# The first MLP product of a spectral MLP kernel, computed as seven block products of 256 tokens

## The chip, the cores and the metric

The kernel runs on one core of one Trainium2 chip. The metric is device time in microseconds; several executions of the same program are timed, and the median is given. One further execution is recorded by the hardware profiler. Its engines are PE (TensorE, the matrix multiplier; its weight loads are listed apart as PEld), DVE (VectorE), ACT (ScalarE), POOL (GpSimd) and SP (SyncE, which issues transfers). Each engine runs its own queue of instructions in order and waits on the others by semaphores. All matmul results land in PSUM, which has eight banks of 512 float32 columns on 128 partitions; ACT and DVE read them from there.

## The reference

The reference takes eight sequences of 3008 tokens with 256 features through a spectral filter, and then every token through an MLP of two layers (hidden width 2048, leaky ReLU):

```python
X = np.fft.rfft(x, axis=1)
Yr = Xr @ w_r - Xi @ w_i + b_r
Yi = Xr @ w_i + Xi @ w_r + b_i
# soft threshold 0.01 on both, then
y = np.fft.irfft(Y, n=x.shape[1], axis=1)
...
h = x @ w_in                    # x: 24064 x 256, w_in: 256 x 2048
g = np.maximum(0.01 * h, h)
return (g @ w_out)              # w_out: 2048 x 256
```

## The kernel before

The Fourier transform of length 3008 = 47 x 64 is done by matmuls. For each of the eight sequences (`b`) there are three stages, which hand on through DRAM: `fwd(b)` (transform of length 47: load `xin`, fold, multiply by `fa`, store to `u_dram`), `mid(b)` (transform of length 64 by `fb` in `stage_b`, the two complex products with the filter in `proj`, soft threshold, back by `gb` in `stage_g`, store to `v_dram`) and, inside the MLP, `inverse` (back transform of length 47 by `ga`). For accuracy every float32 operand is split into a high and a low part (`_hi`, `_lo`, `gh`, `gl`, `yh`, `yl`: the high part is a cast to float32r, the low part the rest), and every product is done by three matmuls: high by high, high by low, low by high (`products`). The weights `w_in` and `w_out` come as float64 bits and are converted on chip (`convert_win`, `load_wout`).

The MLP works on chunks of two column sets: 52 chunks, 44 of them of 470 tokens and 8 of 423 (padded to 424). For each chunk and each of 16 blocks of 128 hidden features (`f`) the function `moe_h` does the first product (six matmuls into one PSUM bank named `psh`), ACT applies the leaky ReLU from PSUM into `gf` (L437) and casts it to `gh` (L438), and DVE forms `gl` (L439). `moe_o` does the second product (six matmuls, L455) three blocks later (`LAG = 3`), accumulating over all 16 blocks into two banks named `pso`. During a chunk, `v_load` and `inverse` make the next chunk's tokens.

The PSUM banks are given out in rotation by name: `psh` has two, `pso` three, `psf` (all other stages) three. The code interleaves the other stages with the MLP by generators: a `Stream` of `fwd(b + 2)` and one of `mid(b + 1)` are advanced a little after each step of the MLP. The code's order is not the final one: a scheduler of the language puts the instructions of each engine in an order of its own, from its own estimates of times, when the program is built. The order then is fixed, and each engine follows it. Ahead of the MLP lie `fwd(0)`, `mid(0)` and `fwd(1)`, and the conversion of the weights; I call this the start.

## Time and profile before

| | |
|---|---|
| Time, median of 3 runs (lowest to highest) | 2699.18 us (2699.11 to 2699.51) |
| Profiled execution: time, span of its instructions | 2699.9 us, 2698.1 us |
| Mean granted TensorE clock | 0.995 |
| PE busy, matmuls recorded | 2651.5 us (98%), 13848 |
| DVE busy, instructions | 1329.4 us (49%), 2447 |
| ACT busy, instructions | 1421.9 us (53%), 2781 |
| POOL busy, instructions | 225.7 us (8%), 180 |
| Mean transfer rate | 61 GB/s |

A matmul's record lasts from its start to its last result, and the next one starts well before that; what a matmul costs in a dense row is therefore the distance from its start to the next start, not its duration. A line of the profile that names a helper (L76, `products`) stands for all its callers, which the tile names tell apart: `psh<-yh,win_hi` is the first MLP product, `pso<-gh,wout_hi` the second. The profiled execution lies 1.8 us above its span and 0.7 us above the median of the timed runs.

### The profile page before, as it was taken

The numbers are of one execution on the slowest core, as the hardware profiler recorded it, in microseconds if no ns is written. First come the engines' busy times: TensorE is split into PE (matmuls) and PEld (weight loads), VectorE is DVE, ScalarE is ACT, GpSimd is POOL, SyncE is SP. The second block draws the span as 40 slices with busy tenths as digits, with TensorE's granted clock in tenths as the row PEclk, the third lists the DMA queues.
The fourth block names the chain that finished last, engine by engine and source line by source line (L and its number), as shares of the span: only waits on it lengthen the run. The fifth ranks groups of instructions, "written<-read, shape, count | busy, mean of one in ns | idle before, by whom it ended". The sixth has DMA issues, their size and how long they took to land.

```text
span 2698.1 us, 36477 instructions
## 1 busy us (share of the span) xinstructions
PE 2651.5 (98%) x13848; PEld 2379.0 (88%) x13848; DVE 1329.4 (49%) x2447; ACT 1421.9 (53%) x2781; POOL 225.7 (8%) x180
## 2 busy tenths in 40 slices
PE   5899999999999999999999999999999999999999
PEld 3688989988898988998889888898889989899888
DVE  6685653555445554455544555445543454433232
ACT  4465555555555555555554555555555555545454
POOL 0011110111101111011100011001000000000000
PEclk8999999999999999999999999999999999999999
DMA  7732222122211212122121221212212011110000
GB/s 221 207 108 64 68 60 69 56 65 59 61 52 56 66 51 71 43 70 61 52 64 42 68 71 48 70 45 67 57 39 60 26 46 39 38 39 27 8 15 14
DMA packets 121260, 164.74 MB, mean 61 GB/s; under 512 B 13697, under 2 KB 83325, under 8 KB 121085
## 3 DMA queue, kind: packets, MB, share of 16 engines
q1 hardware_dynamic: 80640, 116.07, 13.9%
q10 hardware_dynamic: 40445, 46.34, 6.9%
q8 instruction: 109, 1.79, 0.3%
q14 instruction: 66, 0.54, 0.1%
HBM read 86.60 MB, written 75.76 MB: 60 GB/s over the span
## 4 chain that ended last, share of the span: by engine, by line
PE 96%; DMA 1%; DVE 1%; ACT 1%; issue 0%; SPq 0%; ACTq 0%; DVEq 0%
PE psh L76 39%; PE pso L455 39%; PE psf L76 12%; PE psf L407 3%; PE psf L285 3%; PE pso L285 0%; DMA xin<-x_dram 0%; DMA u<-u_dram 0%; PE pso L76 0%; DMA raw<-w_out_dram 0%; ACT xin L233 0%; DMA w_r<-w_r_dram 0%; DMA u_dram<-xin 0%; DVE zf L337 0%; DMA fa<-fa_dram 0%
## 5 line engine op out<-in xcount | busy, mean ns | idle before, releaser
L439 DVE TENSOR_TENSOR gl<-gf,gh 128x470 fp32r<-128x470 f32 (+1 forms) x832 | 557.6, 671 | 1055.0 <-ACT gh L438 978.5
L437 ACT ACTIVATE gf<-psh 128x470 f32<-128x470 f32 (+1 forms) x832 | 464.1, 558 | 847.7 <-PE psh L76 787.1
L76 PE MATMUL psh<-yh,win_hi 128*128 128x470 f32 (+1 forms) x1664 | 636.0, 382 | 0.0
L455 PE MATMUL pso<-gh,wout_lo 128*128 128x470 f32 (+1 forms) x1664 | 621.6, 374 | 0.0
L76 PE MATMUL psh<-yl,win_hi 128*128 128x470 f32 (+1 forms) x1664 | 618.7, 372 | 0.0
L76 PE MATMUL psh<-yh,win_lo 128*128 128x470 f32 (+1 forms) x1664 | 618.2, 371 | 0.0
L455 PE MATMUL pso<-gh,wout_hi 128*128 128x470 f32 (+1 forms) x1664 | 617.3, 372 | 0.0
L455 PE MATMUL pso<-gl,wout_hi 128*128 128x470 f32 (+1 forms) x1664 | 604.2, 372 | 4.5 <-DVE gl L439 4.5
L438 ACT CAST gh<-gf 128x470 fp32r<-128x470 f32 (+1 forms) x832 | 483.3, 581 | 25.3 <-ACT gf L437 3.9
L455 PEld LDWEIGHTS pso<-gl,wout_hi 128*128 128x128 f32 x1664 | 312.4, 188 | 41.4 <-DVE gl L439 4.9
L455 PEld LDWEIGHTS pso<-gh,wout_hi 128*128 128x128 f32 x1664 | 312.9, 188 | 37.3
L76 PEld LDWEIGHTS psh<-yh,win_lo 128*128 128x128 f32 x1664 | 313.3, 188 | 35.9
L455 PEld LDWEIGHTS pso<-gh,wout_lo 128*128 128x128 f32 x1664 | 313.1, 188 | 36.0
L76 PEld LDWEIGHTS psh<-yh,win_hi 128*128 128x128 f32 x1664 | 314.0, 189 | 31.2
L76 PEld LDWEIGHTS psh<-yl,win_hi 128*128 128x128 f32 x1664 | 315.7, 190 | 28.9
L319 POOL TENSOR_TENSOR kb<-bias,kc 128x512 f32<-128x512 f32 x84 | 110.8, 1319 | 1437.3 <-ACT kc L316 1350.4
L329 DVE TENSOR_TENSOR t<-psf,kb 64x256 f32<-64x256 f32 x336 | 141.5, 421 | 28.1 <-PE psf L76 24.4
L407 PEld LDWEIGHTS psf<-ga,vin 120*128 120x128 f32 x832 | 116.5, 191 | 12.1 <-issue 4.4
L407 PE MATMUL psf<-ga,vin 120*128 120x128 f32 x832 | 118.0, 275 | 2.5 <-DMA vin<-v_dram 2.4
L212 POOL TENSOR_TENSOR xs<-xin,xin 120x512 f32<-120x512 f32 (+1 forms) x42 | 55.7, 1327 | 564.3 <-DMA xin<-x_dram 327.6
L421 DVE TENSOR_TENSOR yl<-y,yh 128x470 fp32r<-128x470 f32 (+1 forms) x104 | 72.3, 696 | 61.3 <-ACT yh L420 61.0
L345 ACT ACTIVATE zh<-t,sign 128x256 fp32r<-128x256 f32 x168 | 76.7, 503 | 47.8 <-DVE t L331 46.5
(121 smaller groups left out, 2500.5 us busy)
## 6 DMA issues: line engine op xcount, KB each, us to landing
u<-u_dram SPq DMA_DIRECT2D x192, 128.0 KB, 2.7
v_dram<-v ACTq DMA_DIRECT2D x192, 128.0 KB, 2.4
vin<-v_dram SPq DMA_DIRECT2D x96, 240.0 KB, 3.3
xin<-x_dram SPq DMA_DIRECT2D x90, 240.0 KB, 3.0
out_dram<-ob SPq DMA_DIRECT2D x88, 235.0 KB, 2.3
u_dram<-xin ACTq DMA_DIRECT2D x72, 240.0 KB, 2.4
u_dram<-xin SPq DMA_DIRECT2D x24, 240.0 KB, 6.4
win_raw<-w_in_dram SPq DMA_DIRECT2D x4, 1024.0 KB, 7.7
```

The lines of the kernel that those rows point to most:

```text
L76: last = nc.tensor.matmul(dst, a, b, start=(i == 0), stop=(i == len(terms) - 1))
L212: eng.tensor_add(xs, xa, xb)
L285: nc.tensor.matmul(pv[:, dh, :, i, :], u[:, i, s], fbt[:, 0:k + 2:k + 1, :], start=True, stop=True)
L319: pool.tensor_add(kb, bias, kc.unsqueeze(1).broadcast_to([P, 2, D]))
L329: dve.tensor_add(t[64 * r:64 * (r + 1), i, :], ps_y[s, r * D:(r + 1) * D], kb[s, r, :])
L345: act.mul(zh[:, i, :], t[:, i, :], s)
L407: nc.tensor.matmul(py[:, o:o + P], vin[:, c, i, s], consts["ga"][:, c, :], start=True, stop=True)
L421: last = dve.tensor_sub(yl[:, eh, :n], y[:, :n], yh[:, eh, :n].bitcast(F32))
L437: act.activation(gf[:, :n], ph[:, :n], AF.Prelu, alpha=SLOPE)
L438: act.copy(gh[:, :n], gf[:, :n])
L439: dve.tensor_sub(gl[:, :n], gf[:, :n], gh[:, :n].bitcast(F32))
L455: nc.tensor.matmul(po[:, :n], a[:, f, s], r[:, :n], start=(f == 0 and j == 0), stop=(f == NF - 1 and j == 2),)
```

## The change

The first MLP product is regrouped. Chunks now have 512 tokens (47 chunks, which no longer fall together with the column sets, now called pairs). Hidden features are taken two blocks at a time (`q`, 8 steps a chunk). For one step the product of a 2 x 2 block matrix of weights (two blocks of hidden features by two halves of the 256 input features) and a 2 x 2 block matrix of tokens (two halves of the features by two halves of 256 tokens) is computed by seven block products instead of eight. The sums of weight blocks are formed once in `convert_win` (seven forms, `[P, 7, NQ, P]`), the sums of token blocks once per chunk in `forms`. Each block product is three matmuls with 256 columns. With the products called P1 to P7, `moe_a` puts P1 and P6 into the two halves of one bank and P5 and P7 into those of another; ACT copies P1 out (`p1`), DVE adds `u2` = P1 + P6 and `c22` = P7 + `u2` + P5. Then `moe_b` lets TensorE add P2 onto P1, P3 onto P5 and P4 onto P7, and DVE adds `u2` to the latter two. ACT applies the leaky ReLU in three pieces, casts all 1024 columns to `gh`, and DVE forms `gl`. `moe_o` is the second product as before, with 512 columns, and two steps of lag.

PSUM now has three `psh` banks and two `pso` banks; each step takes two `psh` banks, so the first bank of a step is the second bank of the step two before. Many SBUF tiles of different stages now share buffers (one name per group: `e`, `z`, `u`, `v`, `y`, `yc`, `yl`, `gf`, ...). Two of these matter below: the first two input tiles of `fwd(1)` lie in the buffers of `yc`, which `inverse` and `forms` fill and read for the first two chunks; and the output tile `ob`, the tile `y` of `inverse` and the tile `v` of `stage_g` share two buffers. The streams of `fwd` and `mid` are now advanced one after the other, at a rate that spreads them over 95% of a sequence's share of the chunks instead of 75%.

The core of the diff:

```diff
     NPAIR = NK1 // 2
-    NT = 2 * NG * N1
+    NQ = NF // 2
+    NT, HT = 512, 256
+    NV = 2 * NG * N1
...
+    def block(dst, l, r, start=False):
+        for i, (a, b) in enumerate(((l[0], r[0]), (l[0], r[1]), (l[1], r[0]))):
+            nc.tensor.matmul(dst, a, b, start=start and i == 0, stop=i == 2, skip_group_check=True)
...
     def convert_win(c):
         if c == 0:
-            pair("win", [P, NH, DF])
-        s = slice(c * NIN, (c + 1) * NIN)
-        float64_parts(win_raw[c], *(w[:, :, s] for w in consts["win"]), (("vin", 2), ("raw", 3)))
+            pair("win", [P, 7, NQ, P])
+        a, q = float64_parts(win_raw[c], (("vin", 2), ("yh", 2)))
+        dve.tensor_add(a, a, q)
+        a = a.rearrange("p (j q i m) -> p j q i m", j=NH, q=2, i=2)
+        a11, a12, a21, a22 = (a[:, j, :, i] for i in range(2) for j in range(2))
+        s = sb.tile([P, 4, 2, P], F32, name="ws", tag="yh", bufs=2)
+        dve.tensor_add(s[:, 0], a21, a22)
+        dve.tensor_sub(s[:, 2], a11, a21)
+        dve.tensor_sub(s[:, 1], s[:, 0], a11)
+        dve.tensor_sub(s[:, 3], a12, s[:, 1])
+        hi, lo = (w[:, :, 2 * c:2 * c + 2] for w in consts["win"])
+        for k, w in ((slice(0, 2), a[:, :, :, 0]), (2, a22), (slice(3, 7), s)):
+            act.copy(hi[:, k], w)
+            last = dve.tensor_sub(lo[:, k], w, hi[:, k].bitcast(F32))
+        return last
...
-            while len(raws) < min(c + 2 if c < 2 else c + 3, NF // n):
-                raw = sb.tile([P, CS, 2], U32, name="raw", tag="raw", bufs=3)
+            while len(raws) < min(c + 2 if c < 2 else c + 4, NF // n):
                 k = len(raws)
+                raw = sb.tile([P, CS, 2], U32, name="raw", tag="ez"[k % 2])
                 with tc.issue_after(reads[-1].ins):
                     sync.dma_start(raw.rearrange("p (a f) w -> p a (f w)", a=n), ov[:, k * n:(k + 1) * n, :])
...
-            s = slice(c * n, (c + 1) * n)
-            made.append(float64_parts(raws[c], *(w[:, s, :] for w in consts["wout"]), (("cva", 2), ("cvq", 1))))
+            a, q = float64_parts(raws[c], (("u", 3), ("v", 2)))
+            dh, dl = (w[:, c * n:(c + 1) * n, :] for w in consts["wout"])
+            a, q = (t.rearrange("p (a f) -> p a f", a=n) for t in (a, q))
+            act.copy(dh, a)
+            dve.tensor_sub(a, a, dh.bitcast(F32))
+            made.append(dve.tensor_add(dl, a, q))
...
-    XT = [(("xa", 3), ("xb", 3))] * 3 + [(("yh", 2), ("gh", LAG + 1)), (("yl", 2), ("gh", LAG + 1))] * 2
-    XT1 = XT[:3] + [(("gh", LAG + 1),) * 2] * 2 + [(("gl", LAG + 1),) * 2] * 2
+    XT = [("gf", 1)] + [("gl", 2)] * 2 + [("gh", 2)] * 2 + [("yc", 2)] * 2
+    XT1 = [("yc", 2)] * 2 + [("gf", 1)] + [("gh", 2)] * 2 + [("gl", 2)] * 2
...
+        lo = p0[pi]
+        while lo < p0[pi + 1]:
+            ci = lo // NT
+            hi = min((ci + 1) * NT, p0[pi + 1])
+            if ci not in f_t:
+                f_t[ci] = sb.tile([P, NH, NT], F32, name="yc", tag="yc")
+            act.copy(f_t[ci][:, eh, lo - ci * NT:hi - ci * NT], y[:, lo - p0[pi]:hi - p0[pi]])
+            lo = hi
...
+    def forms(ci):
+        y = f_t.pop(ci)
+        b11, b12, b21, b22 = (y[:, j, k * HT:(k + 1) * HT] for j in range(2) for k in range(2))
+        t = sb.tile([P, 2, HT], F32, name="yt", tag="yt", bufs=1)
+        yh, yl = y_t[ci] = tuple(sb.tile([P, 7, HT], F32R, name=n_, tag=n_) for n_ in ("yh", "yl"))
+        def split(k, w):
+            act.copy(yh[:, k], w)
+            return dve.tensor_sub(yl[:, k], w, yh[:, k].bitcast(F32))
+        split(0, b11)
+        split(slice(1, 3), y[:, 1].rearrange("p (k n) -> p k n", k=2))
+        dve.tensor_sub(t[:, 0], b12, b11)
+        dve.tensor_sub(t[:, 1], b22, t[:, 0])
+        dve.tensor_sub(b12, b22, b12)
+        dve.tensor_sub(b11, b21, t[:, 1])
+        split(slice(3, 5), t)
+        last = split(slice(5, 7), y[:, 0].rearrange("p (k n) -> p k n", k=2))
+        if ci == 0:
             made[:] = [last]
-    def moe_h(ci, f):
-        n = t0[ci + 1] - t0[ci]
-        n += n % 2
-        s = slice(f * P, (f + 1) * P)
-        ph = bank("psh", 2)
-        products(ph[:, :n], [
-            (tuple(w[:, kt, s] for w in consts["win"]), tuple(y[:, kt, :n] for y in y_t[ci]))
-            for kt in range(NH)
-        ])
-        gf = sb.tile([P, NT], F32, name="gf", tag="gf")
-        gh = sb.tile([P, NT], F32R, name="gh", tag="gh", bufs=LAG + 1)
-        gl = sb.tile([P, NT], F32R, name="gl", tag="gl", bufs=LAG + 1)
-        act.activation(gf[:, :n], ph[:, :n], AF.Prelu, alpha=SLOPE)
-        act.copy(gh[:, :n], gf[:, :n])
-        dve.tensor_sub(gl[:, :n], gf[:, :n], gh[:, :n].bitcast(F32))
-        g_t[ci, f] = (gh, gl)
...
+    AK = (0, 1, 6, 2, 3, 4, 5)
+    BK = (0, 1, 2, 5, 3, 4, 6)
+    def product(dst, ci, q, k, start=False):
+        block(
+            dst, tuple(w[:, AK[k - 1], q] for w in consts["win"]), tuple(y[:, BK[k - 1]] for y in y_t[ci]), start)
+    def moe_a(ci, q):
+        b1, b2 = bank("psh", 3), bank("psh", 3)
+        lo, hi = slice(0, HT), slice(HT, NT)
+        product(b1[:, lo], ci, q, 1, True)
+        product(b1[:, hi], ci, q, 6)
+        product(b2[:, hi], ci, q, 7, True)
+        product(b2[:, lo], ci, q, 5)
+        p1 = sb.tile([P, HT], F32, name="p1", tag="p1", bufs=1)
+        u2 = sb.tile([P, HT], F32, name="u2", tag="u2", bufs=1)
+        act.copy(p1, b1[:, lo])
+        dve.tensor_add(u2, b1[:, hi], p1)
+        c22 = sb.tile([P, HT], F32, name="c22", tag="p1", bufs=1)
+        dve.tensor_add(c22, b2[:, hi], u2)
+        dve.tensor_add(c22, b2[:, lo], c22)
+        h_t[ci, q] = (b1, b2, u2, c22)
+    def moe_b(ci, q):
+        b1, b2, u2, c22 = h_t.pop((ci, q))
+        lo, hi = slice(0, HT), slice(HT, NT)
+        product(b1[:, lo], ci, q, 2)
+        product(b2[:, lo], ci, q, 3)
+        product(b2[:, hi], ci, q, 4)
+        g = sb.tile([P, 4, HT], F32, name="gf", tag="gf", bufs=1)
+        act.activation(g[:, 3], c22, AF.Prelu, alpha=SLOPE)
+        act.activation(g[:, 0], b1[:, lo], AF.Prelu, alpha=SLOPE)
+        dve.tensor_add(
+            g[:, 1:3], b2.rearrange("p (k n) -> p k n", k=2), u2.unsqueeze(1).broadcast_to([P, 2, HT]))
+        act.activation(g[:, 1:3], g[:, 1:3], AF.Prelu, alpha=SLOPE)
+        gh = sb.tile([P, 4, HT], F32R, name="gh", tag="gh")
+        act.copy(gh, g)
+        gl = sb.tile([P, 4, HT], F32R, name="gl", tag="gl")
+        dve.tensor_sub(gl, g, gh.bitcast(F32))
+        g_t[ci, q] = (gh, gl)
...
+        if q == 0:
+            o_t[ci, eh] = bank("pso", 2)
+        po = o_t[ci, eh]
+        s = slice(eh * P, (eh + 1) * P)
+        for i in range(2):
+            f = 2 * q + i
             for j, (a, r) in enumerate(((wh, gh), (wl, gh), (wh, gl))):
...
+        if q == NQ - 1:
+            ob = sb.tile([P, NT], F32, name="ob", tag="y")
+            act.copy(ob, po)
+            sync.dma_start(out[s, ci * NT:(ci + 1) * NT], ob)
...
-        for i, (ci, f) in enumerate(steps):
-            moe_h(ci, f)
+        for i, (ci, q) in enumerate(steps):
+            moe_a(ci, q)
             if i >= LAG:
-                moe_o(*steps[i - LAG])
+                moe_o(*steps[i - LAG], 0)
+            yield ci + (q + 0.5) / NQ
+            if i >= LAG:
+                moe_o(*steps[i - LAG], 1)
+            moe_b(ci, q)
...
```

Three places show how the change moves instructions. The first is PE in the last chunk, where only the MLP is left. Before, the six matmuls of one first product (the last three are shown) are followed by a second product (numbers tell tiles of one name apart):

```order
L76 MATMUL psh_25152<-yh_24741,win_hi_234 128x424
L76 MATMUL psh_25152<-yl_24742,win_hi_234 128x424
L76 MATMUL psh_25152<-yh_24741,win_lo_235 128x424
L455 MATMUL pso_24935<-gh_25122,wout_hi_739 128x424
L455 MATMUL pso_24935<-gh_25122,wout_lo_740 128x424
L455 MATMUL pso_24939<-gh_25122,wout_hi_739 128x424
L455 MATMUL pso_24939<-gh_25122,wout_lo_740 128x424
L455 MATMUL pso_24935<-gl_25123,wout_hi_739 128x424
```

Now, at the same place, the last product of a step (P4, into `psh_28720`) is followed at once by the first product (P1) of the step two later, into `psh_28821`, which lies in the same bank; P2 of the step between comes behind it:

```order
L84 MATMUL psh_28720<-yh_28391,win_hi_216 128x256
L84 MATMUL psh_28720<-yl_28392,win_hi_216 128x256
L84 MATMUL psh_28720<-yh_28391,win_lo_217 128x256
L84 MATMUL psh_28821<-yh_28391,win_hi_216 128x256
L84 MATMUL psh_28821<-yl_28392,win_hi_216 128x256
L84 MATMUL psh_28821<-yh_28391,win_lo_217 128x256
...
L84 MATMUL psh_28770<-yh_28391,win_hi_216 128x256
L84 MATMUL psh_28770<-yl_28392,win_hi_216 128x256
L84 MATMUL psh_28770<-yh_28391,win_lo_217 128x256
```

What moved: between the last write of a `psh` bank and its first write two steps later PE has nothing else in its queue here; before, a whole second product lay between.

The second place is DVE in the same chunk. Before, DVE has only one instruction for each block of 128 hidden features:

```order
L439 TENSOR_TENSOR gl_25085<-gf_25083,gh_25084 128x424
L439 TENSOR_TENSOR gl_25104<-gf_25102,gh_25103 128x424
L439 TENSOR_TENSOR gl_25123<-gf_25121,gh_25122 128x424
L439 TENSOR_TENSOR gl_25142<-gf_25140,gh_25141 128x424
L439 TENSOR_TENSOR gl_25161<-gf_25159,gh_25160 128x424
```

Now it has five instructions for each step (two blocks):

```order
L503 TENSOR_TENSOR gf_28710<-psh_28669,u2_28683 128x512
L487 TENSOR_TENSOR u2_28734<-psh_28719,p1_28733 128x256
L509 TENSOR_TENSOR gl_28717<-gf_28710,gh_28715 128x1024
L489 TENSOR_TENSOR c22_28737<-psh_28720,u2_28734 128x256
L490 TENSOR_TENSOR c22_28737<-psh_28720,c22_28737 128x256
L503 TENSOR_TENSOR gf_28761<-psh_28720,u2_28734 128x512
L487 TENSOR_TENSOR u2_28785<-psh_28770,p1_28784 128x256
```

What moved: the `gl` of one step (`gl_28717`) stands in the queue between `u2` and `c22` of the next one, so that `c22` waits for it, and with `c22` the products P3 and P4.

The third place is DVE at the end of the start. Before, the additions of `fwd(1)` on the input tiles stand ahead of the additions of `inverse` (`y`) for the first chunks:

```order
L212 TENSOR_TENSOR xs_847<-xin0_799,xin1_801 120x512
L213 TENSOR_TENSOR xin0_799<-xin0_799,xin1_801 120x512
L212 TENSOR_TENSOR xs_858<-xin0_803,xin1_805 120x512
L213 TENSOR_TENSOR xin0_803<-xin0_803,xin1_805 120x512
L212 TENSOR_TENSOR xs_869<-xin0_807,xin1_809 120x256
L213 TENSOR_TENSOR xin0_807<-xin0_807,xin1_809 120x256
L414 TENSOR_TENSOR y_764<-psf_756,odd_763 128x240
L416 TENSOR_TENSOR y_764<-psf_756,odd_763 128x230
```

Now they stand behind `inverse` and `forms` (`yl`) of the first two chunks and the first two conversions of `w_out` (`wout_lo`), directly ahead of the first MLP step's `u2`:

```order
L233 TENSOR_TENSOR xs_876<-xin_847 120x512
L234 TENSOR_TENSOR xin_844<-xin_844 120x512
L234 TENSOR_TENSOR xin_847<-xin_847 120x512
L233 TENSOR_TENSOR xs_887<-xin_850 120x512
L234 TENSOR_TENSOR xin_850<-xin_850 120x512
L233 TENSOR_TENSOR xs_898<-xin_853 120x512
L234 TENSOR_TENSOR xin_853<-xin_853 120x512
L233 TENSOR_TENSOR xs_909<-xin_856 120x512
L234 TENSOR_TENSOR xin_856<-xin_856 120x512
L233 TENSOR_TENSOR xs_920<-xin_859 120x256
L234 TENSOR_TENSOR xin_859<-xin_859 120x256
L487 TENSOR_TENSOR u2_992<-psh_977,p1_991 128x256
```

What moved: from the first conversion of `w_out` to the first `u2` DVE now has 62 instructions in a row, the 14 of `fwd(1)` last.

More of the change, by code (lines that the diff above doesn't have):

```diff
@@ L240, in fwd @@
             load(c)
-        yield 0
+        yield 4 * CS if b >= NPRE else 0
         fold(0)
@@ L278, in stage_b @@
             u = u_t.pop(j)
-            pb = bank("pso", 3) if b < 1 else bank("psf", 3)
+            pb = bank("psh", 3) if b < 1 else bank("psf", 3)
             pv = pb.rearrange("p (a c i k) -> p a c i k", a=NH, c=2, i=2)
@@ L350, in stage_g @@
         def stage_g(j):
-            pg = bank("pso", 3) if b < 1 else bank("psf", 3)
+            pg = bank("psh", 3) if b < 1 else bank("psf", 3)
             last = products(pg, [(consts["gb" if b else "gb32"], tuple(flat(z) for z in z_t.pop(j)))])
@@ L478, in moe @@
         for s in steps[-LAG:]:
-            moe_o(*s)
+            for eh in range(NH):
+                moe_o(*s, eh)
     class Stream:
@@ L641, in _tokens @@
     cols = []
[L642 removed]
+    for c in _pairs(nb):
         n2 = [(b, NS * g + s) for b, s, n in c for g in range(n)]
```

227 lines of the change are left out of this document (106 added, 121 removed).

## The prediction

> **What bounds the kernel now.** I read the page first: shares of the span, slices, the chain that ended last.
>
> ```profile
> span 2698.1 us, 36477 instructions
> PE 2651.5 (98%) x13848; PEld 2379.0 (88%) x13848; DVE 1329.4 (49%) x2447; ACT 1421.9 (53%) x2781; POOL 225.7 (8%) x180
> ...
> PEclk8999999999999999999999999999999999999999
> ...
> PE 96%; DMA 1%; DVE 1%; ACT 1%; issue 0%; SPq 0%; ACTq 0%; DVEq 0%
> ```
>
> PE carries the time: 98% busy, 96% of the chain, at full clock after the first slice. Whether it is dense shows in the windows (length; busy time of PE, PEld, DVE, ACT, POOL; clock; share and rate of transfers):
>
> ```profile
> 0.00:50.00 50.00, 26.61 (x79) 14.97 (x80) 28.21 (x39) 23.86 (x36) 0.52 (x5) 0.83 0.87 274
> 50.00:100.00 50.00, 41.92 (x198) 33.26 (x197) 39.73 (x74) 23.62 (x51) 0.00 (x0) 0.93 0.60 167
> 100.00:150.00 50.00, 38.69 (x154) 26.12 (x153) 37.16 (x68) 25.82 (x53) 5.86 (x5) 0.97 0.66 205
> ...
> 1000.00:1500.00 500.00, 500.00 (x2652) 454.25 (x2650) 241.51 (x453) 265.11 (x524) 48.98 (x39) 1.00 0.20 58
> ```
>
> In the middle PE never idles, and DVE is half busy (241.51 of 500). Only the start has holes. So the time is the MLP's matmuls, and less work on PE is worth its full length as long as nothing else makes PE wait.
>
> **PE work.** Distances between starts in the timeline (start, duration):
>
> ```profile
> 1501.06 0.28 PE L76 MATMUL psf<-wn_hi,eh 128*128 128x256 f32 x1
> ...
> 1501.78 0.37 PE L76 MATMUL psh<-yh,win_hi 128*128 128x470 f32 x1
> ...
> 1503.05 0.38 PE L455 MATMUL pso<-gh,wout_hi 128*128 128x470 f32 x1
> ...
> 1508.30 0.39 PE L76 MATMUL psf<-zh,gb_hi 128*128 128x512 f32 x1
> ...
> 1508.98 0.38 PE L76 MATMUL psh<-yh,win_hi 128*128 128x470 f32 x1
> ```
>
> Six matmuls lie between the first rows: 0.72/6 = 0.120 us with 256 columns; 1.27/6 = 0.212 with 470; three with 512 take 0.68/3 = 0.227. The line through 256 and 470 gives 0.230 at 512 and 0.192 at 424; I take 0.230. Before, the MLP has 44 chunks x 16 x 12 = 8448 matmuls of 470 columns and 1536 of 424: 1791 + 295 = 2086 us. After, 47 chunks x 8 steps x 21 = 7896 of 256 and 4512 of 512: 948 + 1038 = 1986. The change takes off 100 us. Bounds: 0.227 for 512 columns makes it 114, 0.233 makes it 87. All lies on the path. The seven products save an eighth of half the MLP, some 130 us; about 30 go back to the fixed part of twice as many short matmuls.
>
> A short product needs as many weight loads as a long one:
>
> ```profile
> L76 PEld LDWEIGHTS psf<-wn_hi,eh 128*128 128x128 f32 x168 | 31.6, 188 | 2.0
> ```
>
> The load lasts 188 ns, longer than 120, yet the rows above run at 0.120: loads overlap. The Trainium skill ("TensorE: Matmul & The Clock Gate", LDWEIGHTS) gives a load of 128 columns 107 ns. By it a 256-column product is not held up, but any shorter one would be; the 0.120 agrees with that.
>
> **Vector work.** Rows of the nearest forms (busy, mean ns | idle before):
>
> ```profile
> L439 DVE TENSOR_TENSOR gl<-gf,gh 128x470 fp32r<-128x470 f32 x704 | 479.7, 682 | 894.7 <-ACT gh L438 883.0 <-PE psh L76 3.8 <-PE pso L455 3.4
> L298 DVE TENSOR_TENSOR xi<-psf,xi 128x256 f32<-128x256 f32 x84 | 35.7, 425 | 49.2 <-ACT eh L297 46.7
> L299 DVE TENSOR_TENSOR el<-psf,eh 128x512 fp32r<-128x512 f32 x84 | 57.2, 681 | 0.0
> L134 DVE TENSOR_TENSOR win_lo<-cva,cvq 128x1024 fp32r<-128x1024 f32 x4 | 4.9, 1219 | 0.0
> L221 DVE CAST xh<-xin 120x512 fp32r<-120x512 f32 x36 | 22.8, 634 | 11.5 <-PE psf L76 11.1
> L316 ACT COPY kc<-psf 128x256 f32<-128x256 f32 x96 | 35.8, 373 | 38.8 <-PE psf L76 38.0
> L95 ACT CAST wd_hi<-w_d 128x512 fp32r<-128x512 f32 x1 | 0.6, 621 | 0.0
> L132 ACT CAST win_hi<-cva 128x1024 fp32r<-128x1024 f32 x4 | 4.2, 1056 | 4.9 <-DVE cva L128 4.8
> L455 PE MATMUL pso<-gl,wout_hi 128*128 128x470 f32 x1408 | 517.0, 375 | 4.5 <-DVE gl L439 4.5
> ```
>
> DVE per step: `u2` and two `c22` 3 x 0.425, the addition into `gf` 0.681, `gl` 1.219: 3.18 us against 5.28 of PE (21 x 0.120 + 12 x 0.230). That is 376 x 3.18 = 1194 us instead of 558. `forms` adds four subtractions (0.425) and 0.425 + 3 x 0.681 of splits, 4.2 us a chunk or 196; the splits of `inverse` (72 us) go. DVE comes to some 2100 us, 80%. ACT: 0.373 (`p1`), 0.4 and 0.373 and 0.621 (ReLU), 1.056 (cast) are 2.8 a step, 1060 us for 948; with the copies to `yc` and `forms` some 1650, 63%. Neither engine is full over any chunk (some 42 of DVE against 54 of PE), so I cost this throughput at nothing, with PE as its cover. `forms` stands in the queue almost a chunk ahead of its use. What does cost is latency.
>
> **New waits in the steady part.** The handovers, at one block of the MLP:
>
> ```profile
> 2502.42 0.37 PE L76 MATMUL psh<-yh,win_lo 128*128 128x470 f32 x1
> ...
> 2502.83 0.56 ACT L437 ACTIVATE gf<-psh 128x470 f32<-128x470 f32 x1 [1.60 <-PE psh L76]
> ...
> 2503.42 0.59 ACT L438 CAST gh<-gf 128x470 fp32r<-128x470 f32 x1
> ...
> 2504.04 0.65 DVE L439 TENSOR_TENSOR gl<-gf,gh 128x470 fp32r<-128x470 f32 x1 [2.13 <-ACT gh L438]
> ```
>
> An engine starts 0.03 to 0.04 us after the one that it waits for; a 256-column result is there 0.28 - 0.12 = 0.16 after PE went on. Two chains start at P4, the last product of a step:
> - To the bank: 0.16 + 0.04 + 0.68 (addition into `gf`, which empties the bank) + 0.06 back to PE = 0.94 us until P1 of the step two later may write there.
> - To the second product: 0.16 + 0.04 + 0.68 + 0.04 + 0.62 (ReLU) + 0.03 + 1.06 (`gh`) = 2.63 until `gh`, and 0.03 + 1.22 + 0.06 more, 3.94, until `gl` can be used.
>
> In the built order I counted how much PE work (at the distances above) lies between P4 and each of these, for all 376 steps. Of 374 steps with a successor, 42 have nothing between P4 and that P1 (as shown for the last chunk), and 100 have less than 0.94: short by 53 us in all. For `gl` 67 steps have less than 3.94, short by 65 us. The waits of one step cover each other, so I take the largest of each step: 77 us, of which 34 in the last ten chunks, where no stream is left to fill. Before, the wait of a `gl` matmul on DVE cost 4.5 us in all. 77 assumes that no vector instruction waits in its queue. With each 0.3 late (half an instruction of another stage ahead of it) the count gives 135, with 0.6 it gives 209. Below, it could be 40 (the 42 bare places alone), if waits of neighbouring steps cover each other too. `u2` and `gl` ahead of `c22` in DVE's queue make P2, P3 and P4 wait for them, but there the count finds room. I take 95, nearest to 77, because the dense middle leaves a median of 2.9 us for the 0.94 and 5.5 for the 3.94.
>
> **The start.**
>
> ```profile
> 96.32 0.43 DVE L126 TENSOR_SCALAR cva<-cva 128x512 f32<-128x512 f32 x1
> ...
> 100.46 0.68 DVE L130 TENSOR_TENSOR cvq<-cvq,raw 128x512 f32<-128x512 f32 x1
> 101.06 0.69 DVE L133 TENSOR_TENSOR cva<-cva,wout_hi 128x512 f32<-128x512 f32 x1
> ...
> 110.54 0.69 DVE L212 TENSOR_TENSOR xs<-xin,xin 120x512 f32<-120x512 f32 x1
> ...
> 118.44 0.77 SPq L387 DMA_DIRECT2D vin<-v_dram  x2
> ...
> 132.37 0.56 PE L76 MATMUL psh<-yh,win_hi 128*128 128x470 f32 x1
> ...
> 133.53 1.39 DVE L96 TENSOR_TENSOR gb_lo<-gb,gb_hi 128x128 fp32r<-128x128 f32 x1
> ...
> 143.24 0.80 PE L455 MATMUL pso<-gl,wout_hi 128*128 128x470 f32 x2 [4.54 <-DVE gl L439]
> ...
> 145.40 0.59 PE L76 MATMUL psh<-yh,win_hi 128*128 128x470 f32 x1
> 145.79 0.60 PE L76 MATMUL psh<-yl,win_hi 128*128 128x470 f32 x1
> ```
>
> The load of a piece of `w_out` (KB, us to landing):
>
> ```profile
> raw<-w_out_dram SPq DMA_DIRECT2D x8, 512.0 KB, 6.0
> ```
>
> Before, DVE does most of `fwd(1)`'s additions from 110 us on, while PE waits for `vin`, and the MLP starts at 132.4. Now the first `w_out` conversion waits for its load, which SP issues behind `vin`: 118.4 + some 2 + 6.0 puts DVE at about 126. Its block there has 62 instructions: two conversions (each 3 x 0.43 and 4 x 0.68, 4.0), six `inverse` (two of about 0.4), two `forms` (4.2), six splits of constants (3 x 0.68, 1.39 and two no longer), 14 additions (12 x 0.69 and 2 x 0.42): some 36 us of durations, about 31 when independent neighbours overlap by 0.08 (0.68 long, 0.60 apart above). So the first `u2` comes near 156, and P1 waits for the last addition. Up to the eighth `gl` follow 8 x 3.18, six conversions, 12 casts (0.63) and 12 subtractions (0.68) of `fwd(2)`: 65 us, some 60 with the overlap. DVE, not PE, sets the first chunk, until 216. Before, PE had by then done 216 - 132.4 less 4.5 of wait and some 2 of slow clock, about 76 us; now 42 + 6: a loss of 27 us. `convert_win` gains 2.8 a quarter, 11 in all (out: 2 x 1.22; in: 2 x 1.22, 0.68 and 5 x 0.425); they lie in DVE's holes during `mid(0)` (28.21 and 39.73 busy of 50). Bounds: 6 if DVE gets to the block 10 us sooner and the conversions find holes, 40 if `convert_win` delays `mid(0)` in full.
>
> At 145.40 the distance is 0.39 instead of 0.21: after the wait of 4.54 PE ran at half clock. The Trainium skill (same page, Part 1) says that about 3.4 us of idleness halves the clock until PE was busy as long. By it, the first chunk's holes of some 5 us a step would keep PE at half clock there; 48 us of work would need up to 96, past DVE's 90, and the sum would be up to 6 higher. The waits of the steady part, near 1 us, would not trigger it.
>
> **The rest at nothing.** `ob`, `y` and `v` share two buffers and wait for each other's transfers:
>
> ```profile
> out_dram<-ob SPq DMA_DIRECT2D x88, 235.0 KB, 2.3
> ```
>
> 2.3 us on ACT at most once a chunk; the cover is the 2.3 to 2.7 us of PE work which the order leaves between the last use of a `pso` bank and its next. If it is gone, up to 1 us x 47, inside the range. Loads and stores use 61 GB/s and are hidden as before. The tail keeps its form.
>
> **Sum** against the profiled execution (2699.9): 2699.9 - 100 + 95 + 27 = 2722; the median of the runs lies 0.7 lower: 2721.
>
> **Rivals.**
> 1. *The waits cover each other* (faster). For it: PE work moved ahead of P4 in dense chunks leaves medians far above need, and before the queues hardly waited. Against: the 42 bare places are in the order, and in the last ten chunks nothing fills them. Waits 40, start 27: 2666. It decides where new waits and start together fall below 95.
> 2. *Vector queues run late.* DVE at 80% with instructions up to 1.22, in order; each step of the chain 0.6 late gives 209: 2835. Against: `gl` at 0.65 to 0.68 and handovers of 0.04 show prompt queues where they have room. For it: POOL and DMA waits stand in the same queues.
> 3. *Weight loads bind*: 7896 x (0.188 - 0.120) = 537 more, 3258. The row of six at 0.120 speaks against.
> 4. *The saving is smaller*: as 512-column matmuls at 0.233: 2735, inside the forecast.
>
> **Chances.** 0.2% (5.4 us) is about what a measurement of this kernel can tell from no change. Forecast, waits of 77 to 125: 0.48, its own range 2703 to 2752, a little of it within 0.2%. Rival 1: 0.32, of which 0.05 ends within 0.2%. Rival 2: 0.18. Rival 3: 0.02. So faster 0.27, same 0.12, slower 0.61. The range 2668 to 2790 leaves out the far ends of rivals 1 and 2.
>
> **What would show it.** PE work: distances of 0.12 and 0.23 in the dense rows. Waits: PE idle before `psh` released by DVE `gf`, and before `pso` by ACT `gh` or DVE `gl`, some 95 us in all, densest after 2200 us; the last 500 us with PE below 95% busy. Start: the first `psh<-yh` near 155, DVE nearly full from 126 to 216. Wrong if these waits are under 60 us, if DVE's block at the start is shorter, or if the gaps spread over all chunks (rival 2).

## Result and the profile after

The changed kernel takes 2802.3 us (median of four runs, 2799.1 to 2804.5) against 2699.35 before: ratio 1.038, 95% interval 1.0362 to 1.0398. It is 103 us slower, where 22 were forecast. The profiled execution took 2799.1, with a span of 2797.3.

The page of the changed kernel, the lines that answer to those of before:

```profile
span 2797.3 us, 43359 instructions
...
PE 2633.9 (94%) x16272; PEld 2313.2 (83%) x16272; DVE 2014.6 (72%) x3775; ACT 1565.6 (56%) x3275; POOL 247.0 (9%) x180
...
PEclk8879999999999999999999999999999999999999
...
PE 74%; DVE 15%; DMA 4%; ACT 3%; issue 2%; POOL 1%; SPq 0%; ACTq 0%; DVEq 0%; POOLq 0%
```

PE's share of the chain that ended last fell from 96% to 74%; DVE has 15%. The windows say that this is so in the middle too (busy time of PE, PEld, DVE, ACT, POOL):

```profile
100.00:150.00 50.00, 25.71 (x90) 17.28 (x89) 31.42 (x70) 19.91 (x45) 0.30 (x1) 0.67 0.50 143
1000.00:1500.00 500.00, 482.57 (x3038) 428.31 (x3038) 374.33 (x700) 287.65 (x606) 66.48 (x45) 1.00 0.22 64
```

DVE works 374 of 500 us, 75% where 80% were forecast, and yet PE waits. A stretch of the last chunk shows how (timeline):

```profile
2760.01 0.40 PE L522 MATMUL pso<-gh,wout_lo 128*128 128x512 f32 x1
...
2760.94 0.39 PE L522 MATMUL pso<-gh,wout_hi 128*128 128x512 f32 x1
...
2760.97 0.37 ACT L486 COPY p<-psh 128x256 f32<-128x256 f32 x1
...
2762.54 0.29 PE L84 MATMUL psh<-yh,win_hi 128*128 128x256 f32 x1
...
2763.87 0.29 PE L84 MATMUL psh<-yh,win_lo 128*128 128x256 f32 x1
2764.19 0.69 DVE L503 TENSOR_TENSOR gf<-psh,u 128x512 f32<-128x512 f32 x1 [3.71 <-PE psh L84]
...
2764.94 0.39 PE L84 MATMUL psh<-yh,win_hi 128*128 128x256 f32 x1 [0.78 <-DVE gf L503]
2764.99 0.42 DVE L487 TENSOR_TENSOR u<-psh,p 128x256 f32<-128x256 f32 x1
...
2765.44 0.42 DVE L489 TENSOR_TENSOR c<-psh,u 128x256 f32<-128x256 f32 x1
...
2765.90 0.42 DVE L490 TENSOR_TENSOR c<-psh,c 128x256 f32<-128x256 f32 x1
...
2766.38 0.19 PEld L84 LDWEIGHTS psh<-yh,win_hi 128*128 128x128 f32 x1 [0.31 <-DVE c L490]
```

Distances first: four of 512 columns take 0.93 us (0.23 each), eleven of 256 columns 1.33 (0.121 each). So the products run as forecast. Then the two waits. P4 is the last product before the gap. The addition into `gf` starts 0.04 us after P4's result, and P1 (at 2764.94) must wait for it, because it takes the bank that P4 filled. That wait the prediction had. Behind the same addition in DVE's queue stands `u2` of the next step, though its `p1` was ready 3.6 us earlier; then both `c22` additions, and P3 (here its weight load, with which the product starts) waits for the second. That wait the prediction had put at nothing.

For the whole trace I summed PE's waits: the distance from each matmul's start to the next start, less its dense distance (0.1195, 0.193, 0.2125, 0.231 us for 256, 424, 470, 512 columns), where more than 0.06 is left. The built order says which product each wait stands before. Distances stretched by less than 0.06 us stay in the work: kernels with the same matmuls come to 2465 to 2478 us, so the split is good to some 12 us. A distance at half clock counts as a wait.

| us | before | after | difference | forecast |
|---|---|---|---|---|
| PE work (span less waits and the end) | 2584.0 | 2476.8 | -107 | -100 |
| waits in the first 300 us | 90.7 | 135.9 | +45 | +27 |
| waits behind 300 us | 19.2 | 180.8 | +162 | +95 |
| from the last matmul's start to the end | 4.2 | 3.9 | 0 | 0 |

The 180.8 of after: 67.3 before P1 (243 times), 38.2 before a product that reads a new `gh` or `gl` (178), 46.7 before P3 (204) and 3.9 before P2, 1.5 before P4 and P7, 23.3 before other stages' products (the 19.2 of before are of small waits too). The same in the groups of lines, behind 300 us:

```profile
L84 PE MATMUL psh<-yh,win_hi 128*128 128x256 f32 x2518 | 738.7, 294 | 59.4 <-DVE gf L503 34.6 <-DVE c L490 16.5 <-ACT yh L453 0.3
...
L522 PE MATMUL pso<-gh,wout_hi 128*128 128x512 f32 x1445 | 572.8, 396 | 5.7 <-ACT gh L507 5.6
...
L522 PE MATMUL pso<-gl,wout_hi 128*128 128x512 f32 x1445 | 516.8, 398 | 11.6 <-DVE gl L509 11.4
```

These count only the time in which PE has drained, so they are smaller than the lost starts, but the releasers are the same. `p1` comes late, as ACT's groups of the whole run show:

```profile
L501 ACT ACTIVATE gf<-c 128x256 f32<-128x256 f32 x376 | 156.9, 417 | 266.7 <-DVE gl L509 218.2 <-DVE c L490 41.4 <-DVE zh L366 2.8
L502 ACT ACTIVATE gf<-psh 128x256 f32<-128x256 f32 x376 | 141.0, 375 | 231.5 <-DVE gl L509 115.5 <-PE psh L84 110.4 <-DVE c L490 4.4
L486 ACT COPY p<-psh 128x256 f32<-128x256 f32 x376 | 139.0, 370 | 5.7 <-ACT gf L501 0.5 <-PE psh L84 0.4 <-ACT gf L502 0.2
```

The ReLU of `c22` and of P2 write the one `gf`, and so wait 334 us for `gl` of the step before to have read it. The copy `p1` (L486) hardly ever waits itself: it stands behind them. On average it starts 3.0 us after P1's result.

But a late `p1` is seldom what makes `c22` late: `u2` starts some 2 us after `p1` is done, on average. I followed each of the waits before P3 back through DVE's queue, from the second `c22` addition to the last instruction ahead of it that found DVE idle. Of the 46.7 us about 30 end at the addition into `gf` that waits for P4 (as in the stretch above), about 11 at a cast of `fwd` (L242) that waits for POOL, and only about 3 at ACT's ReLUs. One of the second kind:

```profile
1080.44 0.40 PE L522 MATMUL pso<-gh,wout_lo 128*128 128x512 f32 x1
...
1080.67 0.43 DVE L242 CAST xz<-xs 120x512 fp32r<-120x512 f32 x1 [3.26 <-POOL xs L233]
1080.71 1.50 POOL L234 TENSOR_TENSOR xin<-xin,xin 120x512 f32<-120x512 f32 x1
...
1081.34 1.42 DVE L243 TENSOR_TENSOR xz<-xs,xz 120x512 fp32r<-120x512 f32 x1
1082.68 0.41 DVE L490 TENSOR_TENSOR c<-psh,c 128x256 f32<-128x256 f32 x1
...
1083.15 0.58 PE L84 MATMUL psh<-yh,win_hi 128*128 128x256 f32 x1 [2.31 <-DVE c L490]
```

### The profile page after: what moved, and what is told of

It is laid out like the page before. It is cut to its first block, busy times and chain, and to the rows that moved or that the text cites. A ratio compares the mean times of both kernels' runs of the same rounds, so it can differ in the third digit from the quotient of the medians.

```text
span 2797.3 us, 43359 instructions
## 1 busy us (share of the span) xinstructions
PE 2633.9 (94%) x16272; PEld 2313.2 (83%) x16272; DVE 2014.6 (72%) x3775; ACT 1565.6 (56%) x3275; POOL 247.0 (9%) x180
## 4 chain that ended last, share of the span: by engine, by line
PE 74%; DVE 15%; DMA 4%; ACT 3%; issue 2%; POOL 1%; SPq 0%; ACTq 0%; DVEq 0%; POOLq 0%
PE pso L522 33%; PE psh L84 26%; PE psf L78 9%; DVE gf L503 3%; PE psf L428 2%; PE psf L306 2%; DMA xin<-x_dram 2%; DVE gl L509 2%; DVE c L489 2%; DVE c L490 1%; DVE u L487 1%; DVE yl L454 1%; DVE t L349 1%; PE psh L78 1%; DMA u_dram<-xin 1%
## 5 line engine op out<-in xcount | busy, mean ns | idle before, releaser
L84 PE MATMUL psh<-yh,win_hi 128*128 128x256 f32 x2632 | 773.0, 294 | 67.3 <-DVE gf L503 38.3
L84 PE MATMUL psh<-yl,win_hi 128*128 128x256 f32 x2632 | 744.7, 283 | 0.0
L84 PE MATMUL psh<-yh,win_lo 128*128 128x256 f32 x2632 | 743.2, 283 | 0.0
L522 PE MATMUL pso<-gh,wout_hi 128*128 128x512 f32 x1504 | 598.3, 398 | 6.7 <-ACT gh L507 6.6
L522 PE MATMUL pso<-gh,wout_lo 128*128 128x512 f32 x1504 | 593.3, 394 | 0.0
L522 PE MATMUL pso<-gl,wout_hi 128*128 128x512 f32 x1504 | 540.1, 400 | 13.5 <-DVE gl L509 13.3
L509 DVE TENSOR_TENSOR gl<-gf,gh 128x1024 fp32r<-128x1024 f32 x376 | 469.5, 1249 | 99.2 <-ACT gh L507 98.0
L503 DVE TENSOR_TENSOR gf<-psh,u 128x512 f32<-128x512 f32 x376 | 258.9, 688 | 351.2 <-PE psh L84 341.8
L505 ACT ACTIVATE gf<-gf 128x512 f32<-128x512 f32 x376 | 239.0, 636 | 346.0 <-DVE gf L503 335.4
L507 ACT CAST gh<-gf 128x1024 fp32r<-128x1024 f32 x376 | 395.1, 1051 | 10.3 <-ACT gf L505 1.8
```

Source lines behind the costliest of these rows:

```text
L84: nc.tensor.matmul(dst, a, b, start=start and i == 0, stop=i == 2, skip_group_check=True)
L503: dve.tensor_add(g[:, 1:3], b2.rearrange("p (k n) -> p k n", k=2), u2.unsqueeze(1).broadcast_to([P, 2, HT]))
L505: act.activation(g[:, 1:3], g[:, 1:3], AF.Prelu, alpha=SLOPE)
L507: act.copy(gh, g)
L509: dve.tensor_sub(gl, g, gh.bitcast(F32))
L522: nc.tensor.matmul(po, a[:, f, s], r[:, i], start=(f == 0 and j == 0), stop=(f == NF - 1 and j == 2),)
```

## Experiments

Three theories: A, the three `psh` banks with P1 placed right behind P4; B, the one `gf` buffer, which holds ACT and with it `p1` and `c22`; C, queues so full that every handover is late, whatever the buffers. The table gives all runs; the waits are counted as above. With every edit the scheduler builds another order too, except in the two kernels that take the order of the code; so most runs change a cause and the order together.

| kernel | time, us | ratio to before, interval | PE work | waits to 300 | waits behind 300 |
|---|---|---|---|---|---|
| changed kernel | 2802.3 | 1.038 (1.0362-1.0398) | 2477 | 136 | 181 |
| classic_products | 2705.6 | 1.0019 (1.0009-1.0028) | 2573 | 112 | 15 |
| four_banks | 2651.2 | 0.9816 (0.9801-0.9831) | 2465 | 132 | 48 |
| two_gf | 2753.8 | 1.0195 (1.018-1.021) | 2476 | 140 | 134 |
| p1_buffers | 2833.5 | 1.0494 (1.0478-1.0509) | 2476 | 134 | 217 |
| no_gl | 2755.5 | 1.0198 (1.0181-1.0215) | 2467 | 129 | 156 |
| program_order | 2673.7 | 0.9904 (0.9889-0.9918) | 2475 | 129 | 65 |
| early_fwd1 | 2792.5 | 1.0337 (1.032-1.0354) | 2478 | 127 | 185 |
| four_banks_early_fwd1 | 2640.5 | 0.9779 (0.9765-0.9794) | 2465 | 122 | 48 |
| four_banks_two_gf_early | 2641.2 | 0.9782 (0.9768-0.9797) | 2465 | 116 | 54 |
| short_w_out | 2627.8 | 0.9731 (0.9716-0.9745) | 2465 | 109 | 45 |
| late_second_half | 2616.1 | 0.9692 (0.9675-0.9708) | 2469 | 113 | 28 |
| late_second_half_program_order | 2631.9 | 0.9747 (0.9732-0.9761) | 2471 | 124 | 30 |

**classic_products**: the chunks, shared buffers and streams without the seven products.

```diff
-        b1, b2 = bank("psh", 3), bank("psh", 3)
-        product(b1[:, lo], ci, q, 1, True)
...
+        b = bank("psh", 3)
+        products(b, [
+            (tuple(w[:, 2 * i + j, q] for w in consts["win"]), tuple(y[:, j] for y in y_t[ci])) for j in range(NH)
+        ])
```

> The eight classical block products, as 12 matmuls with 512 columns and one bank for each block of hidden features, in everything else as the changed kernel: chunks of 512 tokens, shared buffers, streams, two steps of lag, one gf. No u2, c22 or sums of blocks. If the chains of the seven products make the waits: PE work 100 us more, waits behind 300 us under 40, start at most 30 late, time 2710-2750. Rival (shared buffers, chunks or streams make the waits): waits stay at 120-180 and the time is 2830-2900.

15 us of waits behind 300 us, fewer than before, and 2705.6, a little under the range. By itself the rest of the change makes no steady waits; the 162 come only with the seven products. It does cost 21 us of the 45 at the start.

**four_banks** (the same edit at every `psh` and `psf` bank):

```diff
-        b1, b2 = bank("psh", 3), bank("psh", 3)
+        b1, b2 = bank("psh", 4), bank("psh", 4)
...
-            ps_k, ps_y = bank("psf", 3), bank("psf", 3)
+            ps_k, ps_y = bank("psf", 2), bank("psf", 2)
```

> Four psh banks and two psf banks, so that the first bank of a step is the first bank of the step two before, released by the ReLU of P2 and no longer by the addition behind P4. Theory A (the three banks: PE must wait for the bank that P4 filled last, and the order leaves too little behind it): PE's waits behind 300 us fall from 180 to 40-80 us, of which psf's third bank costs the most, time 2660-2720. Theory B (one gf buffer: the ReLU of the next step and with it p1, u2 and c22 wait for gl): the waits on gf's addition go, those on c22 and gl stay or grow, waits 110-150, time 2735-2775. Theory C (DVE and ACT too full with the other stages, every handover late, whatever the buffers): waits move to other tiles, time 2780-2810.

2651.2, a little below theory A's 2660 to 2720, and 1.8% below before. Groups behind 300 us, and a window:

```profile
L84 PE MATMUL psh<-yh,win_hi 128*128 128x256 f32 x2502 | 704.0, 289 | 1.5 <-DVE u L487 0.6
...
L522 PE MATMUL pso<-gl,wout_hi 128*128 128x512 f32 x1440 | 530.2, 397 | 5.1 <-DVE gl L509 5.0
```

```profile
1000.00:1500.00 500.00, 495.85 (x3201) 448.12 (x3200) 395.86 (x732) 305.06 (x635) 63.94 (x47) 1.00 0.23 65
```

DVE is busier (396 of 500) than in the changed kernel, and PE has its 496. So a full DVE is not the cause by itself (theory C falls). The waits before P1 went from 67 to 3.5 us and those before P3 from 47 to 6: with the fourth bank the scheduler also builds another order, in which a median of 6.3 us of PE work lies between P5 and P3 instead of 3.9. The third bank of `psf` was worth nothing that shows.

**two_gf**:

```diff
-        vin = sb.tile([PA, 2, 2, D], F32, name="vin", tag="vin")
+        vin = sb.tile([PA, 2, 2, D], F32, name="vin", tag="vin", bufs=1)
-        g = sb.tile([P, 4, HT], F32, name="gf", tag="gf", bufs=1)
+        g = sb.tile([P, 4, HT], F32, name="gf", tag="gf", bufs=2)
```

> Two buffers for gf, paid for with vin (one buffer). Theory A (banks): ACT no longer waits for gl (333 us in the changed kernel before the ReLU rows of gf), but PE's waits on gf's addition stay at 80-100 us; the order's bare count of PE waits goes from 77 to 46, time 2755-2790. Theory B (one gf buffer): PE's waits on c22 (57 us) fall under 15 and the others halve; waits behind 300 us 60-90, time 2690-2730. Theory C (full queues): 2785-2810.

```profile
L501 ACT ACTIVATE gf<-c 128x256 f32<-128x256 f32 x376 | 156.3, 416 | 85.6 <-DVE c L490 81.2 <-issue 1.3 <-DVE xz L242 0.4
L502 ACT ACTIVATE gf<-psh 128x256 f32<-128x256 f32 x376 | 144.3, 384 | 147.8 <-PE psh L84 139.6 <-DVE gl L509 2.9 <-DVE c L490 2.8
```

ACT's wait for `gl` is gone (334 to 3 us), `p1` starts 2.1 us after P1 instead of 3.0, and PE's waits before P3 halve (47 to 23). Those before P1 fall less (67 to 52). The time lies at the edge of theory A's. Theory B is not shown even for half of the wait before P3: followed back as above, the waits that end at the addition into `gf` fell from 30 to 17 us and those at the cast that waits for POOL from 11 to 3, and neither waits for the `gf` buffer. The other built order can have done this.

**p1_buffers** (also one buffer for `vin`):

```diff
-        p1 = sb.tile([P, HT], F32, name="p1", tag="p1", bufs=1)
-        u2 = sb.tile([P, HT], F32, name="u2", tag="u2", bufs=1)
+        p1 = sb.tile([P, HT], F32, name="p1", tag="p1", bufs=3)
+        u2 = sb.tile([P, HT], F32, name="u2", tag="u2", bufs=2)
...
-        c22 = sb.tile([P, HT], F32, name="c22", tag="p1", bufs=1)
+        c22 = sb.tile([P, HT], F32, name="c22", tag="p1", bufs=3)
```

> The changed kernel with three psh banks, one gf, and three buffers for p1 and c22, two for u2 (vin one). In the changed kernel p1 comes 3.0 us after P1 on average and PE waits 47 us before P3 for c22. If the shared buffers make p1 and c22 late: the waits before P3 fall under 20 and the time to 2765-2785. If it is ACT's queue (the ReLU of c22, which waits for gl, stands ahead of p1): waits before P3 of 30-45, time 2785-2805. The order's count of PE work that is missing behind P4 stays near 80 us, so the waits on the bank, gh and gl stay at 90-110.

Both expectations missed: 2833.5.

```profile
L522 PE MATMUL pso<-gh,wout_hi 128*128 128x512 f32 x1504 | 607.0, 404 | 51.0 <-ACT gh L507 49.8
...
L486 ACT COPY p<-psh 128x256 f32<-128x256 f32 x376 | 139.9, 372 | 148.6 <-PE psh L84 145.5 <-ACT v L376 0.7 <-ACT gh L507 0.4
```

`p1` is now prompt (0.7 us after P1; it waits for PE, not behind the ReLUs), and the waits before P3 halve to 21; those before P1 fall to about 20. But the scheduler's new order has the first half of a step run ahead, and the additions into `gf` start 1.7 us after P4 on average instead of 0.5: the waits for `gh` and `gl` go from 38 to 138. The waits moved from one place to the next.

**no_gl** (leaves out the low part of `g`):

```diff
-        gl = sb.tile([P, 4, HT], F32R, name="gl", tag="gl")
-        dve.tensor_sub(gl, g, gh.bitcast(F32))
-        g_t[ci, q] = (gh, gl)
+        g_t[ci, q] = (gh, gh)
```

> The subtraction that forms gl is left out, and the third matmul of the second product reads gh instead: DVE does 470 us less, PE the same work. If the late handovers come from DVE's load (72% busy, gl of 1.25 us in front of the additions that PE waits for): the waits behind 300 us fall from 180 to 60-90 though the three banks stay, time 2680-2725. If the banks and their place in the order are enough by themselves: waits 120-150, time 2740-2770. If DVE's load has no part in it: 2785 or more.

470 us less on DVE take only 25 of the 181 us away. The profiled execution is 42 us shorter: these 25, 7 at the start, and 10 that the count holds as work. The additions into `gf` do start sooner (0.25 us after P4 on average instead of 0.52), but 44 us stay before P1 and 43 before P3; of the 43, about 29 still end at the addition into `gf` and 9 at the cast that waits for POOL. DVE's load has a part, and the smaller one.

**program_order**:

```diff
-    with tile.TileContext(nc, schedule_with_timeline_sim=True) as tc:
+    with tile.TileContext(nc) as tc:
```

> The changed kernel with its three psh banks, but with every engine's instructions in the order of the code instead of the scheduler's. In this order 3 of 374 steps have less than 0.94 us of PE work between P4 and the product that needs its bank (100 in the scheduler's order), 4 instead of 67 too little before gl. Theory A1 (the place that the scheduler gives P1, right behind P4, makes the waits; the third bank is enough for another order): PE's waits on gf's addition fall from 97 to under 30 and the MLP products wait little; other stages, which the code puts in lumps, may wait instead. Time 2650-2750. Theory A2 (three banks are too few in any order): those waits stay over 80, time over 2790. If the other stages' stalls outweigh: time over 2790 with waits on psf and not on psh.

2673.7 with three banks: theory A1. Behind 300 us:

```profile
L84 PE MATMUL psh<-yh,win_hi 128*128 128x256 f32 x2502 | 720.0, 289 | 24.0 <-DVE c L490 12.4 <-DVE u L487 9.8
...
L522 PE MATMUL pso<-gl,wout_hi 128*128 128x512 f32 x1437 | 563.8, 392 | 0.1
```

Before P1 4 us are left, for `gh` and `gl` 5; what is left stands before P3 and P2 (47), 3.9 us of PE work behind P5. For the two chains from P4 it is the place in the order that counts. That the fourth bank helps by allowing another order fits this, but is not shown: no run has four banks with the order unchanged.

**early_fwd1**, **four_banks_early_fwd1**, **four_banks_two_gf_early** (the first edit alone, with four banks, and with four banks and two `gf`):

```diff
+    fp.finish()
     for p in due[0]:
         v_load(p)
     wout = load_wout()
...
     forms(0)
-    fp.finish()
```

> fwd(1) is written ahead of the conversion of w_out and of the first inverse, so that DVE does its additions during mid(0), as in the kernel before. If the start cost the 40-45 us that the work done by 300 us shows, and DVE's block at 125-215 us is why: first psh<-yh product before 145 us, time 2755-2770, waits behind 300 us unchanged near 180. Rival: the conversions of w_out and the splits keep DVE full in the first chunk anyway: time 2785-2802.

> Four psh banks and fwd(1) early. The two changes touch different places (steady part, start), so their gains should add: 2651 less 10 is 2641 (2635-2647). If the freed steady part hid some of the start's loss, no more than 2648-2655.

> Four psh banks, two gf buffers (vin one), fwd(1) early. With four banks PE waits some 50 us behind 300 us. If ACT's wait for gl (310 us before the ReLU of c22) sets what is left: 2610-2630. If that idle time costs nothing once there are four banks: 2638-2650; the single vin buffer could cost a few us more.

The edit gains 10 us with three banks and 11 with four, so start and steady part add. The first product came at 136.0 us instead of 158.5, but the rival held: the first chunk is still slow. In early_fwd1:

```profile
140.00:183.00 43.00, 27.60 (x106) 22.16 (x106) 43.00 (x91) 25.48 (x48) 0.39 (x1) 0.67 0.29 90
```

DVE has 43.00 of 43 us. The second `gf` with four banks gains nothing (6 us less wait at the start, 6 more later): the idle time of ACT, an engine that is not the bound, costs nothing once PE has something else to do.

**short_w_out** (on four_banks_early_fwd1):

```diff
-            a, q = float64_parts(raws[c], (("u", 3), ("v", 2)))
+            a = sb.tile([P, CS], F32, name="cva", tag="u", bufs=3)
+            q = sb.tile([P, CS], F32, name="cvq", tag="v", bufs=2)
+            act.mul(q, raws[c][:, :, 0], 2.0 ** -52)
+            act.activation(a, raws[c][:, :, 1].bitcast(F32), AF.Abs, scale=2.0 ** 16)
```

> Four banks and fwd(1) early, and of each w_out conversion five of seven DVE instructions are left out (the limits, the shift, the sign, the mask and the product of the low word): 8 x 2.2 us less on DVE, ACT and PE as before. If DVE's queue sets the first chunk: the 18 us come back on PE, time 2620-2630. If the chains of the first steps or the half clock set it, whatever DVE does: 2634-2642.

12.6 us of 18 come back on PE. So DVE's queue sets most of the first chunk.

**late_second_half** and the same in program order (on four_banks_early_fwd1; also three buffers for `p1` and `c22`, two for `u2`, one for `vin`):

```diff
             moe_a(ci, q)
-            if i >= LAG:
-                moe_o(*steps[i - LAG], 0)
+            if i:
+                moe_b(*steps[i - 1])
             yield ci + (q + 0.5) / NQ
             if i >= LAG:
+                moe_o(*steps[i - LAG], 0)
                 moe_o(*steps[i - LAG], 1)
-            moe_b(ci, q)
```

> Four psh banks, fwd(1) early, three buffers for p1 and c22, two for u2 (vin one), and the code takes P2, P3 and P4 of a step behind P1, P6, P7 and P5 of the next one. In the scheduler's order 2 of 374 steps then have too little work behind P4 for a bank, and the median of PE work between P5 and P3 is 6.6 us. What is left behind 300 us with four banks is 48 us, of which some 16 are there in any order (classic products). If distance is all: 25-35 us, time 2620-2632. If not: 2636-2650.

> The same in the order of the code. The code keeps P5 to P3 a whole step apart too. In program order with three banks PE waited 65 us behind 300 us, 47 of them for c22 and u2 before P3 and P2. Those should go: 15-30 us left, time 2615-2635. If the other stages' lumps stall PE with two psf banks: 2640-2680.

2616.1 is the fastest, 3.1% under before and 4 us below the range. Its page and two windows:

```profile
PE 2549.0 (97%) x16272; PEld 2296.8 (88%) x16272; DVE 2013.9 (77%) x3775; ACT 1591.1 (61%) x3275; POOL 241.9 (9%) x180
...
PE 88%; DVE 6%; DMA 3%; ACT 1%; issue 1%; POOL 0%; SPq 0%; ACTq 0%; POOLq 0%; DVEq 0%
```

```profile
160.00:220.00 60.00, 55.02 (x311) 46.36 (x312) 56.23 (x93) 34.17 (x65) 15.82 (x10) 1.00 0.34 97
1000.00:1500.00 500.00, 499.87 (x3251) 455.58 (x3250) 401.59 (x746) 313.74 (x650) 64.41 (x47) 1.00 0.24 66
```

The additions into `gf` start 0.46 us after P4 on average, almost as late as in the changed kernel (0.52), and PE waits 28 us instead of 181. Late handovers are harmless where a step's worth of other products lies between. The program order of this code is as dense behind 300 us (30), and loses 11 us at the start. The first chunk, where DVE is busy 56 of 60 us, is what is left: 113 us of waits in the first 300 against 91 before.

## Why the prediction was wrong

The direction was right; the sum was 81 us short, because the waits (95 + 27) were 207.

1. *PE work, -100*: right. The difference is -107, within 87 to 114; the median distances of the MLP's matmuls alone give -106.
2. *Vector throughput at nothing*: right in the main. DVE's 72% and ACT's 56% were forecast as 80% and 63%, and four_banks has PE at 496 of 500 with DVE busier. It was not quite nothing: no_gl, with 470 us less on DVE, gave back 42 us, 25 of them steady waits.
3. *New waits, +95*: this step failed, at 162. The two chains from P4 that it counted came to 67.3 + 38.2 = 105.5 us, near the 95. That is in part luck: the count took the vector queues as prompt, and the addition into `gf` was 0.5 us late on average, where the prediction's own count gives 135 us for 0.3 late at each step of the chain and 209 for 0.6. The failed step is the sentence that P2, P3 and P4 also wait for `u2` and `c22`, "but there the count finds room", which put this wait at nothing. With the prediction's bare handovers P5 to P3 takes 0.16 + 0.04 + 0.42 + 0.06, some 0.7 us, and the built order leaves 1.08 at least and 3.9 in the median. In the trace the second `c22` addition starts 2.2 us after P5's result on average and takes 0.4, because DVE works in order: ahead of it stand the addition that waits for P4 (about 30 us of PE's waits) and a cast that waits for POOL (about 11). That is 46.7 us before P3 and 3.9 before P2. In the order of the code, with the same 3.9 us of distance, 47 us stay there; with a step's worth of products between (late_second_half and the same in the order of the code) some 30 us are left in all, and `u2` and `c22` end next to none of them.
4. *The start, +27*: too small, +45, beyond its upper bound of 40. The first product came at 158.5 where 155 was forecast, and DVE did set most of the first chunk (short_w_out, early_fwd1). But 21 of the 45 come without the seven products (classic_products, whose waits to 300 us are 112 against 91), and 24 from them; the 27 was a sum of DVE's block and the first chunk with no loss ahead of 132 us, where PE had also done 4 us less work.
5. *Half clock, up to +6*: the mechanism is there, and the size is near. Windows of the changed kernel, the last one from its steady part:

```profile
160.00:180.00 20.00, 13.23 (x61) 10.98 (x61) 16.97 (x36) 11.73 (x23) 0.00 (x0) 0.74 0.43 136
180.00:200.00 20.00, 15.63 (x72) 12.08 (x70) 17.72 (x31) 9.17 (x16) 6.27 (x4) 0.83 0.23 62
200.00:220.00 20.00, 18.32 (x97) 15.07 (x98) 16.34 (x28) 9.59 (x19) 6.41 (x5) 1.00 0.49 136
...
1083.00:1086.40 3.40, 3.25 (x11) 2.84 (x12) 3.37 (x4) 1.19 (x4) 2.36 (x2) 0.50 0.18 57
```

The clock was 0.74 and 0.83 up to 200 us and full from there to 300. No run prices it alone, but the distances of the matmuls that started at half clock do: they exceed the dense ones by 6.4 us in the first chunk (158 to 220 us), and by 5.9 between 100 and 158 us, against 1.5 before. So some 11 of the 45 us at the start are half clock. In the steady part, where the prediction expected none, three waits were followed by 3.4 us at half clock, some 4 us lost in all: the one of 2.31 us shown above, one of 1.98 and one of 2.52; two more of 2.1 us were not. The waits near 1 us did not lower it. The Trainium skill ("TensorE: Matmul & The Clock Gate", Part 1) has the clock halved after an idle window of about 3.4 us; here shorter waits were followed by it, and the measurement decides.

6. *Shared output buffers at nothing*: not tested alone; classic_products has them, and only 15 us of steady waits.

Of the rivals, 2 (late queues, 2835) came nearest in its time, and the gaps did spread over all chunks (30 to 37 us of waits in each 500 us from 300 to 1800). Its reason, instructions that stand in order ahead of the chain, is what the waits before P3 show. For the chains from P4 it holds in part only: the first link was 0.5 us late, but in late_second_half it is 0.46 late and costs next to nothing, because the order puts more between. Rival 3 (weight loads) is excluded by the 0.121 us. A faster outcome was within reach of the seven products, not by waits that cover each other (rival 1) but by one bank and the order of the code: four_banks and late_second_half.

## What to carry to other kernels

When a product is split into a chain through other engines, count for every handover of the chain, also those with slack, how much work of the bounding engine lies between, and compare it with the handover as queues make it (here 0.7 us bare and 2.8 real), not with the sum of bare durations. The cure is distance, by one more PSUM bank or by taking the second half of a step behind the first half of the next one; making a helper engine lighter or giving it one more buffer, without looking first at what stands ahead in the queue, moved the wait (p1_buffers) or took a seventh to a quarter of it (no_gl, two_gf). A scheduler's built order should be read for places with nothing in between, and run against the order of the code.

## What the hardware showed beside this

A subtraction on DVE that reads two SBUF tiles took 1.65 us instead of 0.68 when POOL was at work. From early_fwd1 (timeline of POOL, then of DVE):

```profile
183.97 1.52 POOL L234 TENSOR_TENSOR xin<-xin,xin 120x512 f32<-120x512 f32 x1
```

```profile
184.39 1.65 DVE L243 TENSOR_TENSOR xz<-xs,xz 120x512 fp32r<-120x512 f32 x1
...
190.37 0.68 DVE L243 TENSOR_TENSOR xz<-xs,xz 120x512 fp32r<-120x512 f32 x1
```

The slow one ends 0.55 us after POOL's, as if it had started only then. The Trainium skill ("SBUF — State Buffer", SBUF: two separate sides) describes such a lock between the two engines; these rows agree with it. The steady part feels it too: behind 300 us the changed kernel has 15 such subtractions (`xz<-xs,xz`) beside a POOL instruction, and 13 of them took 1.2 to 1.7 us, where none of the 20 others took over 0.68. One stands in the chain shown above (1.42 us at 1081.34), ahead of the `c22` that P3 waits for.
